# One core, attention and two gated layers in one kernel: normalising sums in two broadcasts, own buffer rings for the heads, and order edges behind the step's main work

## The chip, the cores and the metric

The kernel runs on 1 core of one Trainium2 chip. The metric is the device time of one execution in microseconds (us). The core has five engines with a queue each, worked off in order: TensorE (PE; its weight loads are shown as PEld), VectorE (DVE), ScalarE (ACT), GpSimd (POOL) and SyncE (SP), which here only issues DMAs.

## The reference, cut to what matters

Batch 4, 8 heads, sequence 1152, head size 64. Queries are pooled in pairs, so 576 remain.

```python
q_pool = q.reshape(B, H, S // 2, 2, D).mean(axis=3)
attn = softmax(q_pool @ k.T / 8)            # per head, 576 x 1152
x = concat_heads(attn @ v)                  # (4, 576, 512)
# stage 2: 4 experts of size 64, the best 2 of 4 per token weigh in
for e in range(4):
    a = softmax(causal(x @ wq[e] @ (x @ wk[e]).T / 8))
    out += gate[..., e] * (a @ (x @ wv[e]) @ wo[e])
# stage 3: previous token mixed in, then two products and a gate
k = relu(xk @ w_k); out = sigmoid(xr @ w_r) * (k * k @ w_v)
```

## The kernel before, in words

**Order of the work.** The code emits steps (`Step`: `qk` for the products on PE, `ew` and `ew2` for what follows on other engines, `pv` for the value products). `drive` (L168) goes through the list of steps; a step's `pv` runs LAG = 4 steps later. Side work is put in between: `Task(start, end, atoms)` spreads a list of small functions over a stretch of steps, and `later(n, f)` runs f n steps on. What is emitted is not yet the order on the engines: the framework's scheduler sorts all instructions at compile time with its own estimate of durations, and may put an instruction whose inputs it believes ready ahead of others that were emitted long before. `behind(ins, prev)` (L760) adds an edge without a semaphore (`NoSync`), which holds `ins` behind `prev` in that order.

**Stage 1** (`s1_job`, L767) has 32 heads of 9 steps, some 26 us each. A step multiplies one block of 128 keys with all 576 queries (L781, L782) into one of two score buffers `st`, and ACT takes the exponential (L787) into one of 10 buffers `p`. POOL and DVE add the `p` of a head up (L797, L801). Value products (L815) run after steps 2, 5 and 8 of a head; ACT copies the result out of PSUM into `U` (L824). In the next head the summed `p` is multiplied with ones (L831), and `finish2` (L846) copies these sums of the softmax into the other half of `U` (L848). A DMA spreads them over 64 partitions (`sd`, L854), DVE takes the reciprocal (L858), a DMA writes them to memory (`scr`, L859), a DMA broadcasts them back (`R`, L863: 2 groups of 64 partitions with 288 values each), and POOL multiplies `U` by `R` into `XT` (L871). `mid`, `bcast` and `end` are run by `later`, 1, 2 and 5 steps after the sums. Heads 0 and 1 take another way (`finish`, L876, and `normaliser`, L237, whose broadcast goes to 64 partitions with 576 values, L254).

For the head after next, `s1_prep` (L620) transposes keys and queries and splits them into a high and a low part (`sk`), and DMAs copy these into `KK` and `QQ` (L668, L669, L711, L712); `s1_max` (L719) multiplies again for the maximum of each row, which DVE takes (L730); `max_finish` (L393) sends it to `QQ` by DMA (L409, L410). All of these results, and the value products, share four PSUM banks (`aux`, L117).

**Stage 2** of a batch runs inside the next batch's heads: `s2_split` (L259) copies `XT` to `XH` on ACT and subtracts on DVE for `XL` (one pair of heads at a time), `s2_vproj` (L267) and `s2_qk` (L337) project, `s2_max` and `s2_job` (L419, L455) do an expert, whose end (`normaliser`, L237; `end`, L533) goes like a head's, with `mid`, `bcast` and `end` 2, 3 and 4 steps after the sums; `s2_out` (L545) is the output projection. Where these steps stand among a head's nine is written out by hand in `G` (L26): `p1` for three steps of `s2_vproj` and one of `s2_qk` in head 1 of the next batch, `po` for `s2_out` in head 0 of the batch after. The task of `s2_split` comes at step 13 counted from the start of the next batch's head 0 (L1089). The last batch's stage 2 and the weights' last chunks follow from 817 us on.

**Stage 3** reads weights that `w3_split` (L938) makes out of float64 words, in 20 chunks through one staging buffer `w3st`: a load (L947), seven small steps on DVE and ACT (L960 to L990), two stores (L993). It fills the last 226 us.

U, R, `sd` and `rd` of heads and experts come from one pool `sm` with two buffers a name.

Of the kernel before, what the change touches and what calls it, by code (L numbers as in the profile page):

```python
# [9 lines left out]
F32 = mybir.dt.float32  # L10
# [5 lines left out]
ALU = mybir.AluOpType  # L16
# [39 lines left out]
def tile_kernel(ctx: ExitStack, tc: tile.TileContext, q, k, v, w_gate, wq, wk, wv, wo,  # L56
# [5 lines left out]
    def copy(e, dst, src):  # L62
        if e == "s":
            nc.scalar.activation(dst, src, AF.Copy)  # L64
        elif e == "v":
            nc.vector.tensor_copy(dst, src)
        else:
            nc.gpsimd.tensor_scalar(dst, src, 1.0, 0.0, op0=ALU.mult, op1=ALU.add)

    def lo_of(e, dst, src, hi):  # L70
        eng[e].tensor_tensor(dst, src, hi.bitcast(F32), op=ALU.subtract)  # L71

# [80 lines left out]
    def later(n, fn):  # L153
        pending.append((now[0] + n, fn))
# [10 lines left out]

    lagged = []

    def drive(steps, tasks, drain=False, first=0):  # L168
# [67 lines left out]

    def normaliser(U, gate, name):  # L237
# [217 lines left out]
    def s2_job(pp, b, e):  # L455
# [68 lines left out]
        def finish(j):  # L524
            if j == 0:
                acc["U"] = sm.tile([P, T], F32, tag="U", name=f"U{name}")
            U = acc["U"]
            copy_eps(G["u2"], U[: D + 1, j * HT : (j + 1) * HT], acc[j][: D + 1, :HT])
            if j == 0:
                return  # L530
            mid, R = normaliser(U, GR[:, e], name)

            def end():  # L533
                o0 = (e % 2) * D
                y = U
                eng[G["y2"]].tensor_tensor(y[o0 : o0 + D], U[0:D], R, op=ALU.mult)
                copy(G["yh"], YH[o0 : o0 + D, e // 2], y[o0 : o0 + D])
# [68 lines left out]
    def s1_load(hh):  # L606
        b, h = hh // H, hh % H
        kr = s1a.tile([P, NC * D], F32, tag="kr", name=f"kr{hh}")
        qr = s1a.tile([QW, NQ, 2, D], F32, tag="qr", name=f"qr{hh}")
        raw[hh] = kr, qr  # L610
        return [
            lambda: nc.sync.dma_start(qr, q[b, h].rearrange("(c p r) d -> p c r d", p=QW, r=2)),
            lambda: nc.sync.dma_start(kr, k[b, h].rearrange("(p c) d -> p (c d)", p=P)),
        ]

    def s1_vload(hh):
        b, h = hh // H, hh % H
        return [lambda: nc.sync.dma_start(VF[hh % NF][:, :, 0:D], v[b, h].rearrange("(p c) d -> p c d", p=P))]

# [99 lines left out]
    def s1_max(hh):  # L719
# [3 lines left out]
        def one(c, g):  # L723
            t0, n = TC[c]

            def f():
                ps = aux()
                nc.tensor.matmul(ps[:n, : 3 * P], QA[i][:, t0 : t0 + n], KA[i][:, 3 * g * P : 3 * (g + 1) * P],  # L728
                                 start=True, stop=True)
                nc.vector.tensor_reduce(pm[:n, c, g : g + 1], ps[:n, : 3 * P], axis=AX.X, op=ALU.max)  # L730
            return f
# [27 lines left out]

    def behind(ins, prev):  # L760
        if prev is not None:
            tc.add_manual_dep(ins.ins, prev.ins.name,
                              mybir.DependencyInfo(mybir.DependencyClass.NoSync, mybir.DependencyReason.DATA),
                              reason="order")
        return ins

    def s1_job(hh):  # L767
# [5 lines left out]
        def make(si):  # L773
# [11 lines left out]
            def ew():  # L785
                pt = ps[si] = pp1.tile([P, 2, HT], F32, tag="p", name=f"p1_{hh}_{si}", bufs=G["PB"])
                nc.scalar.activation(pt, acc.pop(("st", si))[:, :, :HT], AF.Exp, scale=1.0 / 16.0)  # L787

            def ew2():
# [5 lines left out]
                if x is not None:  # L795
                    s = pp1.tile([P, 2, HT], F32, tag="s" + e, name=f"s{e}1_{hh}_{si}", bufs=HB)
                    eng[e].tensor_tensor(s, x, ps[si], op=ALU.add)  # L797
                    sums[e] = s
# [5 lines left out]
            def values():  # L804
# [16 lines left out]
                if si == NC - 1:  # L821
                    owed.append(total)
                    U = acc["U"] = sm.tile([P, T], F32, tag="U", name=f"U1_{hh}")
                    copy("s", U[:, :HT], a[:, :HT])  # L824
                    if hh == NH - 1:
                        owed.pop(0)(last_qk[0])
# [19 lines left out]
        def finish2(s):  # L846
            U = acc["U"]
            nc.scalar.activation(U[0 : D + 1, HT:], s[0 : D + 1, :HT], AF.Identity, bias=eps[0 : D + 1])  # L848
            sd = sm.tile([D, T // D], F32, tag="sd", name=f"sd1_{hh}")
            rd = sm.tile([D, T // D], F32, tag="rd", name=f"rd1_{hh}")  # L850
            scr = dscr.tile([1, T], F32, tag="scr", name=f"scr1_{hh}")
            R = sm.tile([P, HT], F32, tag="R", name=f"R1_{hh}")
            for j in range(2):
# [3 lines left out]
            def mid():  # L857
                nc.vector.reciprocal(rd, sd)  # L858
                nc.sync.dma_start(scr.rearrange("o (p i) -> (o p) i", p=D), rd)  # L859
                later(G["bc"], bcast)  # L860

            def bcast():
                nc.sync.dma_start(R, bass.AP(tensor=scr.tensor, offset=scr.offset, ap=[[HT, 2], [0, D], [1, HT]]))  # L863

            def end():
                o0 = (h % 2) * D
                for j in range(2):
                    a = slice(j * D, (j + 1) * D)
                    x = XT[o0 : o0 + D, h // 2].rearrange("p (t e n) -> p e t n", n=QW, e=2)[:, j]
                    y, z = (w[a].rearrange("p (t n) -> p t n", n=QW) for w in (U[:, :HT], R))  # L870
                    eng[G["xt" if b else "xt0"]].tensor_tensor(x, y, z, op=ALU.mult)  # L871

            later(G["mid"], mid)
            later(G["end1"], end)

# [62 lines left out]
    def w3_split(first, end, pool, bufs):  # L938
        def chunk(src, n):
# [47 lines left out]
            def sp7():  # L987
# [390 lines left out]
```

## Time and profile before

| what | value |
|---|---|
| median of 3 runs | 1174.4 us (1164.23 to 1182.01) |
| the profiled execution | 1168.17 us |
| its span, first to last instruction | 1166.5 us |
| mean granted clock of PE | 0.931 |
| PE, DVE, ACT, POOL busy | 1032.9, 743.9, 456.9, 383.3 us |

Busy time is time in which an engine executes; a wait is the idle time of an engine before an instruction, with the instruction that released it. The clock is the share of PE's full 2.4 GHz that was granted, and 0.50 stands for 1.2 GHz.

### The profile page before, as it was taken

The page shows a single profiled execution, that of the slowest core. Times are in us where ns is not written, and L with a number is a line of the kernel's source. Part 1 is how long each engine was busy: PE and PEld are TensorE (multiplying, and loading weights), DVE is VectorE, ACT ScalarE, POOL GpSimd, SP SyncE. Part 2 cuts the span into 40 slices and gives each one's busy share as a digit, 9 for nine tenths or more (in the row PEclk, how much of TensorE's full clock was granted, in tenths as well). Part 3 has the DMA queues.
Part 4 walks back from the last instruction along what each step waited for, and adds up shares of the span by engine and source line. Part 5 has one row for each costly group of instructions (what it writes and reads, how often), then busy time and mean ns, then how long its engine had stood idle before and what let it go on. Part 6 is the DMA issues. An engine that isn't in the chain of part 4 may idle for free. (4 is left out here: it accounts for less than half of the span.)

```text
span 1166.5 us, 17687 instructions
## 1 busy us (share of the span) xinstructions
PE 1032.9 (89%) x6186; PEld 811.2 (70%) x6186; DVE 743.9 (64%) x1501; ACT 456.9 (39%) x823; POOL 383.3 (33%) x483
## 2 busy tenths in 40 slices
PE   6998877879988789998889899998788899999998
PEld 4765555657666567766667776766776678888887
DVE  5676655576769577786867766684587644444432
ACT  5334334334445433453543434453256322222221
POOL 5156345233334442453433244434212101111110
PEclk9999888889899898998989888997889989999999
DMA  5656464445454474654536455316626421111100
GB/s 132 145 122 143 103 135 107 111 119 118 119 140 111 105 188 118 134 134 119 138 84 180 126 124 120 74 38 190 179 83 194 137 84 37 37 37 37 43 31 19
DMA packets 139655, 128.05 MB, mean 110 GB/s; under 512 B 64741, under 2 KB 103838, under 8 KB 139566
## 3 DMA queue, kind: packets, MB, share of 16 engines
q1 hardware_dynamic: 139566, 126.92, 43.8%
q8 instruction: 49, 0.80, 0.3%
q14 instruction: 40, 0.33, 0.1%
HBM read 63.24 MB, written 20.07 MB: 71 GB/s over the span
## 5 line engine op out<-in xcount | busy, mean ns | idle before, releaser
L730 DVE TENSOR_REDUCE PM<-bank 128x1 f32<-128x384 f32 (+1 forms) x390 | 205.9, 548 | 85.4 <-PE bank L728 83.6
L787 ACT ACTIVATE p<-st 128x576 f32<-128x576 f32 x288 | 184.7, 649 | 135.9 <-PE st L782 129.8
L781 PE MATMUL st<-QQ,KK 128*128 128x288 f32 x576 | 190.1, 341 | 17.4 <-ACT p L787 15.2
L728 PE MATMUL bank<-KK,QQ 128*128 128x384 f32 (+1 forms) x390 | 153.7, 419 | 42.4 <-DVE PM L730 17.7
L782 PE MATMUL st<-QQ,KK 65*128 65x288 f32 x576 | 178.3, 321 | 5.8 <-DMA QQ<-mr 5.2
L797 POOL TENSOR_TENSOR sg<-sg,p 128x576 f32<-128x576 f32 x90 | 137.1, 1523 | 117.4 <-ACT p L787 69.1
L815 PE MATMUL bank<-p,VF 128*64 128x288 f32 x1080 | 165.3, 448 | 0.0
L781 PEld LDWEIGHTS st<-QQ,KK 128*128 128x128 f32 x576 | 118.9, 207 | 41.1 <-ACT p L787 29.1
L728 PEld LDWEIGHTS bank<-KK,QQ 128*128 128x128 f32 (+1 forms) x390 | 77.6, 204 | 77.3 <-DVE PM L730 29.5
L782 PEld LDWEIGHTS st<-QQ,KK 65*128 65x128 f32 x576 | 119.8, 208 | 13.9 <-DMA QQ<-mr 5.9
L815 PEld LDWEIGHTS bank<-p,VF 128*64 128x64 f32 x1080 | 76.0, 148 | 60.2 <-issue 26.4
L871 POOL TENSOR_TENSOR XT<-U,R 64x288 f32<-64x288 f32 x60 | 49.9, 831 | 159.4 <-DMA R<-scr 140.6
L1175 PE MATMUL sth<-xkh,wk 128*128 128x256 f32 x512 | 91.4, 279 | 1.2 <-ACT relu L1182 1.2
L1175 PEld LDWEIGHTS sth<-xkh,wk 128*128 128x128 f32 x512 | 78.7, 188 | 1.8 <-ACT relu L1182 1.4
L503 PE MATMUL bank<-p,V 128*65 128x288 f32 (+5 forms) x288 | 65.9, 364 | 13.1 <-ACT U L64 6.1
L1112 POOL TENSOR_SCALAR yxr<-x,omr 128x256 f32<-128x256 f32 x36 | 26.2, 744 | 140.6 <-DVE xkl L144 130.6
L1175 PE MATMUL sth<-xkl,wk 128*128 128x256 f32 x256 | 71.4, 279 | 0.0
L797 DVE TENSOR_TENSOR sv<-sv,p 128x576 f32<-128x576 f32 x60 | 55.2, 920 | 23.1 <-PE bank L831 12.9
L489 POOL TENSOR_SCALAR_AFFINE_SELECT p<-p 128x128 f32<-128x128 f32 (+1 forms) x96 | 29.3, 336 | 115.9 <-ACT p L481 90.8
L1182 ACT ACTIVATE relu<-sth 128x512 f32<-128x512 f32 x32 | 17.5, 596 | 123.2 <-PE sth L1175 122.5
L797 POOL TENSOR_TENSOR sg<-p,p 128x576 f32<-128x576 f32 x30 | 46.4, 1546 | 52.9 <-ACT p L787 50.3
L1183 DVE TENSOR_TENSOR relu<-relu 128x512 f32<-128x512 f32 x32 | 20.9, 688 | 57.9 <-ACT relu L1182 57.9
(214 smaller groups left out, 2173.1 us busy)
## 6 DMA issues: line engine op xcount, KB each, us to landing
KK<-sk SPq DMA_DIRECT2D x30, 320.0 KB
qr<-in_q_dram SPq DMA_DIRECT2D x32, 288.0 KB
kr<-in_k_dram SPq DMA_DIRECT2D x32, 288.0 KB
VF<-in_v_dram SPq DMA_DIRECT2D x32, 288.0 KB
QQ<-sk SPq DMA_DIRECT2D x60, 144.0 KB
KK<-sk SPq DMA_DIRECT2D x30, 256.0 KB
R<-scr SPq DMA_DIRECT2D x48, 144.0 KB
w3h<-w3st SPq DMA_DIRECT2D x20, 256.0 KB
```

The lines of the kernel that those rows point to most:

```text
L489: nc.gpsimd.affine_select(o, o, pattern=[[1, o.shape[1]]], compare_op=ALU.is_ge, fill=0.0, base=m0, channel_multiplier=-1)
L503: nc.tensor.matmul(a[:, q0 + lo : q0 + hi], V2[:n, c, e], pt[:n, c0 + lo : c0 + hi], start=start, stop=stop)
L728: nc.tensor.matmul(ps[:n, : 3 * P], QA[i][:, t0 : t0 + n], KA[i][:, 3 * g * P : 3 * (g + 1) * P], start=True, stop=True)
L730: nc.vector.tensor_reduce(pm[:n, c, g : g + 1], ps[:n, : 3 * P], axis=AX.X, op=ALU.max)
L781: nc.tensor.matmul(st[:, n, :HT], KA[i][:, ks], QA[i][:, cs], start=True, stop=False)
L782: last_qk[0] = nc.tensor.matmul(st[:, n, :HT], KB[i][0 : D + 1, ks], QB[i][0 : D + 1, cs], start=False, stop=True)
L787: nc.scalar.activation(pt, acc.pop(("st", si))[:, :, :HT], AF.Exp, scale=1.0 / 16.0)
L797: eng[e].tensor_tensor(s, x, ps[si], op=ALU.add)
L815: prev = behind(nc.tensor.matmul(a[j * D : (j + 1) * D, :HT], V[:, x, 0:D], ps[x][:, j], start=si == GRP[0] and x == si, stop=si == NC - 1 ...
L871: eng[G["xt" if b else "xt0"]].tensor_tensor(x, y, z, op=ALU.mult)
L1112: nc.gpsimd.tensor_scalar(y[:, c], t[:, c, 0:GT], om[:, c : c + 1], 0.0, op0=ALU.mult, op1=ALU.add)
L1175: nc.tensor.matmul(st[:, f // 2, f % 2 * GT : (f % 2 + 1) * GT], w[kt][:, fs], x[:, kt], start=i == 0, stop=i == 3 * KT - 1)
```

## The change

Six things are done. (1) The broadcast of `finish2` is two DMAs of 64 partitions each. (2) U, `sd`, `rd` and R of heads come from the pool `pp1`, two buffers a name, and no longer share those of stage 2. (3) For all heads but the last, `mid`, `bcast` and `end` come 2, 4 and 7 steps after the sums; for experts of all batches but the last 3, 5 and 7. (4) `s2_split` is taken apart: the four pairs are copied at steps 1 and 5 of head 6, step 6 of head 7 and step 6 of the next batch's head 1, and the steps of `p1` and `po` come later. (5) `pin` ties instructions without a semaphore behind the latest exponential ("s"), the latest maximum of `s1_max` ("v") or POOL's latest add ("g"): copies out of PSUM, XH and YH copies, reciprocals, products, and the loads of q, k and v. (6) A chunk of `w3_split` has four empty atoms between its load and its first step. Of the last head and the last batch nothing is pinned or put off.

```diff
-G = {... 'mid': 1, 'bc': 1, 'end1': 5, 'mid2': 2, 'end2': 4, 'spl': 9, 'p1': (5, 5, 5, 9), 'po': (2, 4, 5, 9) ...}
+G = {... 'mid': 2, 'bc': 2, 'end1': 7, 'mid2': 2, 'end2': 4, 'mid3': 3, 'end3': 7, 'xhp': ((6, 1), (6, 5), (7, 6), (9, 6)), 'p1': (8, 8, 9, 9), 'po': (4, 5, 7, 9) ...}
+    mark = {}
+    def pin(ins, e):
+        return behind(ins, mark.get(e))
     def normaliser(U, gate, name, pinned=False):
...
-            nc.vector.reciprocal(rd, sd)
+            x = nc.vector.reciprocal(rd, sd)
+            if pinned:
+                pin(x, "v")
...
-            later(G["bc"], bcast)
+            later(G["bc"] if pinned else 1, bcast)
     def s2_split(b):
-                copy(G["xh"], XH[:, p], XT[:, p])
+                x = copy(G["xh"], XH[:, p], XT[:, p])
+                if b < B - 1:
+                    pin(x, "s")
     # s2_job, end: product pinned "v", YH copy pinned "s" if b < B - 1
-            later(G["mid2"], mid)
-            later(G["end2"], end)
+            later(G["mid3" if early else "mid2"], mid)
+            later(G["end3" if early else "end2"], end)
     # s1_load, s1_vload
-            lambda: nc.sync.dma_start(qr, ...),
+            lambda: pin(nc.sync.dma_start(qr, ...), "s"),
     # s1_max, s1_job: the instructions that are tied behind
+                mark["v"] = nc.vector.tensor_reduce(pm[:n, c, g : g + 1], ...)
+                mark["s"] = nc.scalar.activation(pt, ..., AF.Exp, scale=1.0 / 16.0)
+                    mark[e] = eng[e].tensor_tensor(s, x, ps[si], op=ALU.add)
     # values, finish2
-                    U = acc["U"] = sm.tile([P, T], F32, tag="U", name=f"U1_{hh}")
-                    copy("s", U[:, :HT], a[:, :HT])
+                    U = acc["U"] = pp1.tile([P, T], F32, tag="U", name=f"U1_{hh}", bufs=2)
+                    x = copy("s", U[:, :HT], a[:, :HT])
+                    if hh < NH - 1:
+                        pin(x, "s")
...
-                nc.sync.dma_start(R, bass.AP(tensor=scr.tensor, offset=scr.offset, ap=[[HT, 2], [0, D], [1, HT]]))
+                for j in range(2):
+                    nc.sync.dma_start(R[j * D : (j + 1) * D], bass.AP(tensor=scr.tensor, offset=scr.offset + j * HT, ap=[[0, D], [1, HT]]))
...
-            later(G["mid"], mid)
-            later(G["end1"], end)
+            later(G["mid"] if late else 1, mid)
+            later(G["end1"] if late else 5, end)
     # w3_split
-            return [ld, sp1, sp2, sp3, sp4, sp5, sp6, sp7]
+            idle = lambda: None
+            return [ld, idle, idle, idle, idle, sp1, sp2, sp3, sp4, sp5, sp6, sp7]
     # the task of s2_split
-        tasks.append(Task(at(b * H, LAG + G["spl"]), at(b * H, LAG + G["spl"] + 1), s2_split(b - 1)))
+        for f, (i, j) in zip(s2_split(b - 1), G["xhp"]):
+            tasks.append(Task(at((b - 1) * H + i, j), at((b - 1) * H + i, j) + 0.5, [f]))
```

## Rows read from the trace of the kernel before

**Rows 1.** The page: busy us, share of the span, instructions.
```profile
PE 1032.9 (89%) x6186; PEld 811.2 (70%) x6186; DVE 743.9 (64%) x1501; ACT 456.9 (39%) x823; POOL 383.3 (33%) x483
```

**Rows 2.** Waits of PE by releaser: us in total, times, longest us.
```profile
PE bank L728 <- DVE PM L730: 17.7, 16, 5.5
PE st L781 <- ACT p L787: 15.2, 10, 5.2
PE stv L280 <- ACT p L787: 7.5, 2, 3.9
PE bank L728 <- DMA KK<-sk: 6.3, 3, 3.3
PE bank L503 <- ACT U L64: 6.1, 1, 6.1
...
PE st L782 <- DMA QQ<-mr: 5.2, 2, 3.4
PE bank L728 <- ACT U L133: 5.1, 3, 3.0
...
PE stv L280 <- ACT XH L64: 4.8, 2, 3.3
...
PE bank L728 <- ACT U L64: 3.3, 1, 3.3
```

**Rows 3.** Timeline 166.9 to 178: start, us, instruction, [idle before <- releaser].
```profile
166.97 0.58 SPq L863 DMA_DIRECT2D R<-scr  x1
...
174.89 1.63 POOL L871 TENSOR_TENSOR XT<-U,R 64x288 f32<-64x288 f32 x2 [3.98 <-DMA R<-scr]
176.55 0.68 ACT L64 ACTIVATE XH<-XT 128x576 fp32r<-128x576 f32 x1 [4.94 <-POOL XT L871]
177.14 0.63 ACT L787 ACTIVATE p<-st 128x576 f32<-128x576 f32 x1
...
177.83 0.61 PE L781 MATMUL st<-QQ,KK 128*128 128x288 f32 x1 [5.24 <-ACT p L787]
```

**Rows 4.** Waits of POOL and ACT, whole run, as in rows 2.
```profile
POOL XT L871 <- DMA R<-scr: 140.6, 27, 9.6
...
ACT p L787 <- PE st L782: 129.8, 164, 4.4
...
ACT XH L64 <- POOL XT L871: 39.9, 9, 6.9
```

**Rows 5.** Timeline 810 to 814: stage 2's broadcast and its reader.
```profile
810.27 0.53 SPq L254 DMA_DIRECT2D R<-scr  x1
...
813.76 0.75 DVE L536 TENSOR_TENSOR U<-U,R 64x576 f32<-64x576 f32 x1 [1.42 <-DMA R<-scr]
```

**Rows 6.** Timeline 145 to 160: a copy of keys behind an R.
```profile
147.25 0.60 SPq L669 DMA_DIRECT2D KK<-sk  x1
...
155.57 0.66 PE L728 MATMUL bank<-KK,QQ 128*128 128x384 f32 x1 [3.29 <-DMA KK<-sk]
```

**Rows 7.** Timeline 236 to 252: DVE at a weight chunk.
```profile
244.08 0.43 DVE L961 TENSOR_SCALAR w3st<-w3st 128x512 int32<-128x512 int32 x1 [3.38 <-DMA w3st<-in_moe_w_k_dram]
```

**Rows 8.** The chain that ended last, 817 to 836: start, us, what.
```profile
826.39 6.95 DMA R<-scr
```

**Rows 9.** Fifteen half-clock stretches, sum row: us, then busy us by engine.
```profile
sum 95.50, PE 79.75 PEld 59.38 DVE 55.42 ACT 33.27 POOL 35.96; mean PE 5.32 PEld 3.96 DVE 3.69 ACT 2.22 POOL 2.40
```

**Rows 10.** Stretches: us, busy us (instructions) of PE, PEld, DVE, ACT, POOL; clock; DMA.
```profile
105.00:237.00 132.00, 108.56 (x646) 77.07 (x646) 77.33 (x150) 50.46 (x91) 54.44 (x52) 0.90 0.51 114
237.00:466.00 229.00, 196.61 (x1208) 150.12 (x1206) 166.01 (x346) 97.53 (x182) 87.27 (x101) 0.90 0.54 128
466.00:670.00 204.00, 181.21 (x1148) 139.08 (x1149) 150.58 (x318) 90.57 (x170) 79.30 (x93) 0.94 0.55 131
670.00:817.00 147.00, 134.60 (x825) 98.23 (x824) 99.49 (x206) 64.94 (x120) 61.71 (x79) 0.91 0.46 110
455.00:535.00 80.00, 73.10 (x471) 54.02 (x470) 63.90 (x137) 36.13 (x68) 32.94 (x40) 0.98 0.62 137
```

More of the change, by code (lines that the diff above doesn't have):

```diff
@@ new lines @@
+G = {'LAG': 4, 'LO': 2, 'nf1': 2, 'nfx': 1, 'mxA': (0, 5), 'mxB': (-1.0, 5.5), 'mxC': (-3.5, 5.0), 'prA': (0.5, 5.0), 'prB': (-1.5, 2.0), 'mx0': (-4.2, 4.0), 'mx1': (-4.2, 4.0), 'vl': (0.0, 1.5), 'vs': (5.5, 1.0), 'pr0': (-3.0, 1.0), 'pr1': (-3.0, 1.0), 'ldA': (5.5, 5.0), 'ldB': (2.5, 2.0), 'ld': (1.5, 1.0), 'm2': (2.0, 3.0), 'nm': 2, 'nm2': 1, 'dup': 1, 'mid': 2, 'bc': 2, 'end': 9, 'end1': 7, 'mid2': 2, 'end2': 4, 'mid3': 3, 'end3': 7, 'xhp': ((6, 1), (6, 5), (7, 6), (9, 6)), 'gate': 8, 'gate2': 2, 'w2': (2, 30), 'w3': (7, 14), 've': 'g', 'kh0': 's', 'kh1': 's', 'qh0': 's', 'qh1': 's', 'kq': 's', 'kl': 'v', 'rs': 'v', 'rl': 'v', 'ym': 'g', 'yo': 'v', 'LGe': 'v', 'p1': (8, 8, 9, 9), 'p2': (9, 9, 9), 'p3': (2,), 'p4': (9, 9, 9, 9), 'p5': (8, 8, 8, 8), 'p6': (9, 9, 9), 'po': (4, 5, 7, 9), 'add0': 'g', 'add1': 'g', 'xt': 'g', 'u1': 's', 'u2': 's', 'y2': 'v', 'yh': 's', 'yl': 'v', 'xo': 'v', 'v2': 's', 'xh': 's', 'xl': 'v', 'vvh': 's', 'vvl': 'g', 'klo': 'v', 'HB': 2, 'PB': 10, 'GRP': (2, 5, 8), 'GA': (1, 3, 5, 7), 'blk': 1, 'm2w': 2, 'order': 2, 'kdup': 0, 'L2': 4, 'O2': 1, 'a0': (5.0, 5.0), 'a1': (2.0, 2.5), 'a2': (0.0, 1.0), 'a3': (2.0, 2.0), 'r0': 2, 'NV': 2, 'NF': 2, 'ua': 'v', 'u0': 's', 'xt0': 'g', 'w3d': 8, 'w3q': (3, 27), 'WC': 1, 'kb': 1, 'kst': 1, 'qst': 0, 'CW': 512, 'wt': 'v', 'wl': 'v', 'wa': 'v', 'WB': 1, 'mxg': 4, 'hq': 's', 'hpos': (0, 1, 11, 20)}
@@ L63, in copy @@
         if e == "s":
[L64 to L68, printed above, removed]
+            return nc.scalar.activation(dst, src, AF.Copy)
+        if e == "v":
+            return nc.vector.tensor_copy(dst, src)
+        return nc.gpsimd.tensor_scalar(dst, src, 1.0, 0.0, op0=ALU.mult, op1=ALU.add)
     def lo_of(e, dst, src, hi):
-        eng[e].tensor_tensor(dst, src, hi.bitcast(F32), op=ALU.subtract)
+        return eng[e].tensor_tensor(dst, src, hi.bitcast(F32), op=ALU.subtract)
     B, H, S, _ = q.shape
@@ L166, in tile_kernel, with behind @@
     lagged = []
+    mark = {}
+    def behind(ins, prev):
+        if prev is not None:
+            tc.add_manual_dep(ins.ins, prev.ins.name,
+                              mybir.DependencyInfo(mybir.DependencyClass.NoSync, mybir.DependencyReason.DATA),
+                              reason="order")
+        return ins
+    def pin(ins, e):
+        return behind(ins, mark.get(e))
     def drive(steps, tasks, drain=False, first=0):
@@ L235, in tile_kernel, with normaliser @@
     pp_last = None
-    def normaliser(U, gate, name):
+    def normaliser(U, gate, name, pinned=False):
         NI = T // D
@@ L530, in finish @@
                 return
-            mid, R = normaliser(U, GR[:, e], name)
+            early = b < B - 1
+            mid, R = normaliser(U, GR[:, e], name, early)
             def end():
@@ L535, in end @@
                 y = U
-                eng[G["y2"]].tensor_tensor(y[o0 : o0 + D], U[0:D], R, op=ALU.mult)
-                copy(G["yh"], YH[o0 : o0 + D, e // 2], y[o0 : o0 + D])
+                x = eng[G["y2"]].tensor_tensor(y[o0 : o0 + D], U[0:D], R, op=ALU.mult)
+                z = copy(G["yh"], YH[o0 : o0 + D, e // 2], y[o0 : o0 + D])
+                if early:
+                    pin(x, "v")
+                    pin(z, "s")
                 lo_of(G["yl"], YL[o0 : o0 + D, e // 2], y[o0 : o0 + D], YH[o0 : o0 + D, e // 2])
-            later(G["mid2"], mid)
-            later(G["end2"], end)
+            later(G["mid3" if early else "mid2"], mid)
+            later(G["end3" if early else "end2"], end)
         return [make(si) for si in range(3)]
@@ L611, in s1_load @@
         return [
-            lambda: nc.sync.dma_start(qr, q[b, h].rearrange("(c p r) d -> p c r d", p=QW, r=2)),
-            lambda: nc.sync.dma_start(kr, k[b, h].rearrange("(p c) d -> p (c d)", p=P)),
+            lambda: pin(nc.sync.dma_start(qr, q[b, h].rearrange("(c p r) d -> p c r d", p=QW, r=2)), "s"),
+            lambda: pin(nc.sync.dma_start(kr, k[b, h].rearrange("(p c) d -> p (c d)", p=P)), "s"),
         ]
@@ L617, in s1_vload @@
         b, h = hh // H, hh % H
-        return [lambda: nc.sync.dma_start(VF[hh % NF][:, :, 0:D], v[b, h].rearrange("(p c) d -> p c d", p=P))]
+        return [lambda: pin(nc.sync.dma_start(VF[hh % NF][:, :, 0:D], v[b, h].rearrange("(p c) d -> p c d", p=P)), "s")]
     def s1_prep(hh):
@@ L729, in f @@
                                  start=True, stop=True)
-                nc.vector.tensor_reduce(pm[:n, c, g : g + 1], ps[:n, : 3 * P], axis=AX.X, op=ALU.max)
+                mark["v"] = nc.vector.tensor_reduce(pm[:n, c, g : g + 1], ps[:n, : 3 * P], axis=AX.X, op=ALU.max)
             return f
@@ L758, in tile_kernel @@
     last_qk, owed = [None], []
[L760 to L765, printed above, removed]
     def s1_job(hh):
@@ L796, in ew2 @@
                     s = pp1.tile([P, 2, HT], F32, tag="s" + e, name=f"s{e}1_{hh}_{si}", bufs=HB)
-                    eng[e].tensor_tensor(s, x, ps[si], op=ALU.add)
+                    mark[e] = eng[e].tensor_tensor(s, x, ps[si], op=ALU.add)
                     sums[e] = s
@@ L847, in finish2 @@
             U = acc["U"]
-            nc.scalar.activation(U[0 : D + 1, HT:], s[0 : D + 1, :HT], AF.Identity, bias=eps[0 : D + 1])
-            sd = sm.tile([D, T // D], F32, tag="sd", name=f"sd1_{hh}")
-            rd = sm.tile([D, T // D], F32, tag="rd", name=f"rd1_{hh}")
+            late = hh < NH - 1
+            x = nc.scalar.activation(U[0 : D + 1, HT:], s[0 : D + 1, :HT], AF.Identity, bias=eps[0 : D + 1])
+            if late:
+                pin(x, "s")
+            sd = pp1.tile([D, T // D], F32, tag="sd", name=f"sd1_{hh}", bufs=2)
+            rd = pp1.tile([D, T // D], F32, tag="rd", name=f"rd1_{hh}", bufs=2)
             scr = dscr.tile([1, T], F32, tag="scr", name=f"scr1_{hh}")
-            R = sm.tile([P, HT], F32, tag="R", name=f"R1_{hh}")
+            R = pp1.tile([P, HT], F32, tag="R", name=f"R1_{hh}", bufs=2)
             for j in range(2):
@@ L857, in mid @@
             def mid():
-                nc.vector.reciprocal(rd, sd)
+                x = nc.vector.reciprocal(rd, sd)
+                if late:
+                    pin(x, "v")
                 nc.sync.dma_start(scr.rearrange("o (p i) -> (o p) i", p=D), rd)
-                later(G["bc"], bcast)
+                later(G["bc"] if late else 1, bcast)
             def bcast():
-                nc.sync.dma_start(R, bass.AP(tensor=scr.tensor, offset=scr.offset, ap=[[HT, 2], [0, D], [1, HT]]))
+                for j in range(2):
+                    nc.sync.dma_start(R[j * D : (j + 1) * D], bass.AP(tensor=scr.tensor, offset=scr.offset + j * HT, ap=[[0, D], [1, HT]]))
             def end():
@@ L870, in end @@
                     y, z = (w[a].rearrange("p (t n) -> p t n", n=QW) for w in (U[:, :HT], R))
-                    eng[G["xt" if b else "xt0"]].tensor_tensor(x, y, z, op=ALU.mult)
-            later(G["mid"], mid)
-            later(G["end1"], end)
+                    x = eng[G["xt" if b else "xt0"]].tensor_tensor(x, y, z, op=ALU.mult)
+                    if late:
+                        pin(x, "g")
+            later(G["mid"] if late else 1, mid)
+            later(G["end1"] if late else 5, end)
         def finish(j):
```

5 lines of the change are left out of this document (2 added, 3 removed).

## The prediction, before the result was known

> **What bounds the kernel now.** I read the page's busy shares first, then TensorE's own waits, then one of its longest stalls in order of time, then who released the engines in it, and last the stages side by side. TensorE (PE) is busy 89% of the span [rows 1], so only what holds PE up can pay. Of PE's 134 us without work, nine rows of its waits name 71 [rows 2]: ACT is the releaser in six of them (15.2 + 7.5 + 6.1 + 5.1 + 4.8 + 3.3 = 42.0 us), a landing DMA in two (6.3 + 5.2 = 11.5), DVE's maximum in one (17.7).
>
> One stall in full [rows 3]: SP issues the broadcast R<-scr at 166.97; POOL, idle for 3.98, starts the product XT only at 174.89, so the broadcast took about 7.8 us; ACT has the copy XH<-XT at the front of its queue and stands still for 4.94; the exponential behind it starts at 177.14, though its scores were ready; PE, which needs a free score buffer, stood for 5.24. Over the run POOL waits 140.6 us for R and ACT 39.9 for XT in nine copies [rows 4]. POOL's own waiting costs nothing. What ACT passes on does. The code emits this copy only after head 8, and it runs here right behind head 5's product: the scheduler pulled it ahead of exponentials as soon as that product was due by its own reckoning. That is the disease of this kernel: small instructions that wait for a far transfer sit in front of an in-order engine's main work.
>
> **The change, part by part.**
>
> *Broadcast in two.* The 128-partition broadcast takes 7.8 us [rows 3]. The stage-2 one, of as many bytes on 64 partitions out of one row, is issued at 810.27 and releases DVE at 813.76, 3.5 us [rows 5]. Two transfers of 64 partitions are each like it with half the bytes, issued 0.58 apart [rows 3]; bounds 1.8 (half of 3.5) and 7.8 + 0.58; I take 3.5 + 0.6 = 4.1, nearest to the like row, 3.7 less. Price: 30 more issues on SP at 0.58, 17 us of a queue that other DMAs stand in; PE sees them only where the next DMA is one that it waits for.
>
> The Trainium skill, "DMA: Bandwidth & Descriptors", section on the anatomy of one DMA, gives about 2.0 us plus bytes over 436 GB/s (fitted on the POOL path) and advises fewer, larger transfers: an estimate from that page is 2.3 us for the one transfer and 2 x 2.2 for two in series, so the split would lose 2 us per head. The trace disagrees on its first term, 7.8 where the page gives 2.3. The same page, section on why a DMA's semaphore goes up by 16, says that the slowest dimension of both sides sets how many of 16 engines work: 2 before, 16 after; that sides with the 3.5.
>
> *Neighbours of R.* KK<-sk, issued at 147.25, three issues behind an R, released PE at 155.57, 8.3 us [rows 6]. If R leaves its engines 4 us sooner, so does what queues there: the 11.5 us of KK and QQ<-mr. Bounds 0 and 11.5.
>
> *Later middle and end.* In wide heads reciprocal, broadcast and product come 2, 4 and 7 steps after the sums instead of 1, 2 and 5: still three steps from broadcast to product, which at some 26 us per head of 9 to 13 steps are 6 to 8 us, against 4.1. In stage 2 they come at 3, 5, 7 instead of 2, 3, 4: two steps, 4 to 5 us. The last head keeps 1, 2, 5. Results come at most three steps later and are read later still (next point): nothing, with 0 to 3 us at each of three batch ends as bounds.
>
> *XH copies moved and pinned.* The twelve early copies (0.68 each, [rows 3]) go to heads 6, 6, 7 and the second head of the next batch. Head 7's product falls near step 4 of that head, its copy stands at 6, and the projection that reads it goes from 5 to 8: two steps each. No work is added. So the nine ACT stalls [rows 4] lose their cause, but for the last batch's.
>
> *Own rings.* U, sd, rd and R of the heads no longer share two buffers with stage 2. That takes away the evictions U (L133) that waited for XT: 5.1 us of PE [rows 2].
>
> These two parts: 42.0, less 1.4 of stv<-XH that belongs to the unpinned last batch, and 2.4 of st<-p (ten waits, the longest 5.2; my estimate of the short ones in it): 38.2 us. What is late next is the exponential's real input, and DVE.
>
> *Pins on DVE, SP and POOL.* Reciprocals stand behind a maximum, loads behind an exponential, products behind an add. They are order edges without a semaphore, so a load adds no wait at run time; it leaves its place ahead of QQ<-mr in SP's queue. *Idle atoms:* a weight chunk gets four empty slots between its load and its first operation; DVE stood 3.38 us before that operation for the load [rows 7], and a maximum queued behind it. Of DVE's 17.7 I take half, 8.9 (bounds 0 and 17.7): the scheduler may still pull these unpinned operations forward.
>
> *Last head.* Its R is on the chain that ended last, 6.95 us [rows 8]; 4.1 instead gives 2.9.
>
> *The clock.* I took fifteen stretches that begin at or around such gaps and have a granted clock of 0.50, the 1.2 GHz level: 95.5 us together, PE busy in 79.75 of them [rows 9]. At 2.4 GHz the busy part would halve: 39.9 us.
>
> The skill's "TensorE: Matmul & The Clock Gate", section Terms, sets the loss at the throttled time times what is missing of the clock: 47.8 by that estimate, where my row gives 39.9, since PE idled in the rest. The sum would be lower by 4 at half weight.
>
> **Sum.** 38.2 + 11.5 + 8.9 + 2.9 = 61.5 of idle and 39.9 of clock, 101.4 if all is kept. All is not kept, for the stages show a floor [rows 10]. The quietest 80 us (455 to 535, clock 0.98) still idle 6.9, 8.6%. Idle of the stages: 23.4 of 132, 32.4 of 229, 22.8 of 204, 12.4 of 147. Brought to 8.6% they lose 12.0, 12.7, 5.3 and 0: 30, half of 61.5. I keep half of both, 30.7 + 20.0, and take 3 off for the issues and late results: 47.7. From the profiled execution's own 1168.2 (span 1166.5 and 1.7 around it): **1120 us**. The median of three runs is 1174.4; the profiled run is 0.5% faster, so this is 4.6% under the median. About 2% is what a measurement of this kernel tells from no change: 1151 and 1198.
>
> **Rivals.**
>
> *All of it is kept* (10%): 1168.2 - 101.4 = 1067. For it: the stalls named are most of the idle time in 105 to 237. Against: the floor of 8.6%.
>
> *DVE takes over* (17%): the reciprocals pinned behind maxima and the maxima themselves become what PE waits for. For: its maximum is the largest single releaser of PE [rows 2], and each of them has PE queued behind it. Against: over three batches DVE is busy 166 + 151 + 99 of 580 us [rows 10], 72%. Price: half of ACT's and DMA's 49.7 and the last head's 2.9 are won (27.8), the 17.7 of DVE double, the clock drops stay: 1168.2 - 27.8 + 17.7 = 1158.
>
> *Two transfers land no sooner than one* (5%), by whatever holds them: XT still waits, but XH does not stand behind it; half of 38.2 and half of that in clock, 28.7, less 17 of issues: 1157. The skill's rule on batching, named above, would have it so. The change would then not do its first part.
>
> *A pinned eviction holds a bank* (11%): slower. The copies of values and sums out of PSUM (58 in the 29 pinned heads) now stand behind an exponential. That waits for PE's scores, on average 129.8/164 = 0.79 us [rows 4], and takes 0.63 [rows 3]. PE in turn needs one of four banks for its maxima and values (the rows bank<-U in rows 2 show it waiting so). If each passes 1.42 on, that is 82 us: 1120 + 82 = 1202. It decides against the change from 34 of the 58 on (47.7/1.42). Against it: these copies run in step with exponentials already.
>
> *Nothing moves* (2%): 1168.
>
> **How the numbers follow.** The forecast has 55%, with a range of its own of 1095 to 1150 (73 down to 18 of the 101 us kept). Faster by over 2%: 0.53 of the forecast, 0.10, a quarter of the DVE case 0.04 and 0.03 of the two transfers, 0.70. Within 2%: 0.02 + 0.13 + 0.02 + 0.02, 0.19. Slower: 0.11. The range is from 1080 to 1165: it leaves out most of the best case and the slower one.
>
> **What would show it.** Right: the wait XT<-R falls from 140.6 to under 40; ACT's wait XH<-XT is nearly gone; KK no longer appears in PE's waits; the mean granted clock rises from 0.931 to 0.95 or more; PE's rows with ACT as releaser sum to under 20. Wrong: XT<-R stays over 100 (transfers), DVE PM passes 35 in PE's waits (DVE), or bank<-U passes 20 (pins). A clock that stays at 0.93 with less idle time would leave 1140.

## The result and the profile after

The changed kernel takes 1092.66 us (median of four runs, 1089.83 to 1092.99), the kernel before, on the same chip, 1178.2 us (four runs, 1164.23 to 1184.06). The ratio is 0.934, 95% interval 0.927 to 0.941: faster, inside the range of 1080 to 1165, 27 us below the forecast of 1120 and just under the forecast's own range of 1095 to 1150. The ratio compares fast runs alone: two of the four runs of the kernel before, 1182.01 and 1184.06, are over 1.5% above its fastest and are left out, so it isn't the quotient of the two medians. The profiled execution took 1092.36 us.

The page of after, its first line on busy time; the line beside its core gives span and clock:

```profile
PE 999.7 (92%) x6186; PEld 785.7 (72%) x6186; DVE 752.8 (69%) x1501; ACT 454.6 (42%) x823; POOL 396.1 (36%) x483
```

```profile
core 0: 1090.7 us, clock 0.965
```

PE has the same 6186 instructions and is busy 999.7 us instead of 1032.9 [rows 1]. These 33.2 us are put down to the clock (0.931 to 0.965), since the work is the same; 42.6 came from PE's idle time: 1166.5 - 1032.9 = 133.6 before, 1090.7 - 999.7 = 91.0 now. The sum is the 75.8 us that the span lost.

Who still holds PE up, in after's waits of PE by releaser (us in total, times, longest us):

```profile
PE st L792 <- ACT p L798: 7.1, 14, 1.7
PE bank L746 <- DVE PM L748: 6.4, 13, 1.3
PE sth L1259 <- ACT relu L1267: 6.2, 1, 6.2
PE bank L746 <- DVE PM L762: 5.3, 7, 1.8
...
PE bank L517 <- ACT p L495: 4.6, 1, 4.6
...
PE st L793 <- DMA QQ<-ml: 0.2, 1, 0.2
```

Against rows 2: the row of KK<-sk is gone and so is that of QQ<-mr; DVE's maximum fell from 17.7 to 6.4 with a longest wait of 1.3 instead of 5.5; PE's wait for an exponential fell from 15.2 to 7.1. The 6.2 in stage 3 is new, and comes back below.

The same view for POOL and ACT, where rows 4 were 140.6 and 39.9:

```profile
POOL XT L890 <- DMA R<-scr: 52.0, 16, 9.7
...
ACT XH L64 <- POOL XT L890: 3.2, 3, 1.4
```

One broadcast in time order, as the timeline of after shows it (start, us, instruction, idle before it and its releaser). It is to be held against rows 3:

```profile
203.21 1.12 SPq L882 DMA_DIRECT2D R<-scr  x2
...
206.18 0.79 POOL L890 TENSOR_TENSOR XT<-U,R 64x288 f32<-64x288 f32 x1 [1.27 <-DMA R<-scr]
...
207.32 0.79 POOL L890 TENSOR_TENSOR XT<-U,R 64x288 f32<-64x288 f32 x1 [0.36 <-DMA R<-scr]
...
208.15 0.68 ACT L64 ACTIVATE XH<-XT 128x576 fp32r<-128x576 f32 x1 [1.39 <-POOL XT L890]
```

Two issues lie in one row (x2, 1.12 us together). The first half releases POOL 2.97 us after 203.21, the second 4.11 us after it; before, the one transfer took about 7.8 us. ACT stands 1.39 us in front of its copy, where rows 3 show 4.94.

Stretches of after, all in stage 1 (us, busy us and instructions of PE, PEld, DVE, ACT, POOL; clock; DMA share; GB/s):

```profile
105.00:230.00 125.00, 115.68 (x730) 82.68 (x731) 92.89 (x186) 58.99 (x107) 62.96 (x61) 0.97 0.63 145
230.00:445.00 215.00, 202.97 (x1364) 154.78 (x1360) 179.67 (x368) 106.33 (x200) 98.54 (x114) 1.00 0.57 140
445.00:635.00 190.00, 176.26 (x1147) 133.39 (x1148) 157.14 (x316) 88.79 (x167) 86.29 (x93) 0.97 0.58 141
```

In the middle stretch PE idles 215 - 202.97 = 12.0 us, 5.6%, at a clock of 1.00. The 8.6% that the prediction took for a floor [rows 10] was none.

### The profile page after: what moved, and what is told of

Read it like the earlier page. It is cut to its first block, busy times and chain, and to the rows that moved or that the text cites. A ratio compares the mean times of both kernels' runs of the same rounds, so it can differ in the third digit from the quotient of the medians.

```text
span 1090.7 us, 17718 instructions
## 1 busy us (share of the span) xinstructions
PE 999.7 (92%) x6186; PEld 785.7 (72%) x6186; DVE 752.8 (69%) x1501; ACT 454.6 (42%) x823; POOL 396.1 (36%) x483
## 4 chain that ended last, share of the span: by engine, by line
PE 58%; DVE 22%; DMA 9%; ACT 5%; issue 3%; POOL 2%; SPq 1%; DVEq 0%; ACTq 0%; POOLq 0%
PE stw L1234 9%; PE bank L826 8%; PE sth L1198 7%; PE st L792 5%; DVE PM L748 5%; PE bank L746 5%; PE st L793 4%; PE str L1221 4%; PE stq L361 3%; DVE sv L808 2%; PE bank L517 2%; DMA R<-scr 2%; PE bank L853 2%; PE sto L573 2%; DMA scr<-rd 1%
## 5 line engine op out<-in xcount | busy, mean ns | idle before, releaser
L792 PE MATMUL st<-QQ,KK 128*128 128x288 f32 x576 | 182.0, 330 | 10.0 <-ACT p L798 7.1
L793 PE MATMUL st<-QQ,KK 65*128 65x288 f32 x576 | 169.6, 308 | 0.2 <-DMA QQ<-ml 0.2
L808 POOL TENSOR_TENSOR sg<-sg,p 128x576 f32<-128x576 f32 x90 | 134.3, 1492 | 91.0 <-ACT p L798 59.1
L826 PE MATMUL bank<-p,VF 128*64 128x288 f32 x1080 | 155.7, 427 | 0.8 <-DVE PM L748 0.8
L792 PEld LDWEIGHTS st<-QQ,KK 128*128 128x128 f32 x576 | 112.2, 195 | 36.6 <-ACT p L798 19.8
L793 PEld LDWEIGHTS st<-QQ,KK 65*128 65x128 f32 x576 | 112.6, 196 | 7.4 <-issue 4.9
L746 PEld LDWEIGHTS bank<-KK,QQ 128*128 128x128 f32 (+1 forms) x390 | 75.0, 197 | 54.3 <-DVE PM L748 19.6
L826 PEld LDWEIGHTS bank<-p,VF 128*64 128x64 f32 x1080 | 72.2, 141 | 55.2 <-issue 17.8
L890 POOL TENSOR_TENSOR XT<-U,R 64x288 f32<-64x288 f32 x60 | 59.3, 988 | 57.1 <-DMA R<-scr 52.0
L517 PE MATMUL bank<-p,V 128*65 128x288 f32 (+5 forms) x288 | 59.5, 333 | 8.7 <-ACT p L495 4.6
L1206 DVE TENSOR_TENSOR relu<-relu 128x512 f32<-128x512 f32 x32 | 20.8, 687 | 55.9 <-ACT relu L1205 55.9
```

Of the source, the lines that this page charges most:

```text
L517: nc.tensor.matmul(a[:, q0 + lo : q0 + hi], V2[:n, c, e], pt[:n, c0 + lo : c0 + hi], start=start, stop=stop)
L792: nc.tensor.matmul(st[:, n, :HT], KA[i][:, ks], QA[i][:, cs], start=True, stop=False)
L793: last_qk[0] = nc.tensor.matmul(st[:, n, :HT], KB[i][0 : D + 1, ks], QB[i][0 : D + 1, cs], start=False, stop=True)
L808: mark[e] = eng[e].tensor_tensor(s, x, ps[si], op=ALU.add)
L826: prev = behind(nc.tensor.matmul(a[j * D : (j + 1) * D, :HT], V[:, x, 0:D], ps[x][:, j], start=si == GRP[0] and x == si, stop=si == NC - 1 ...
L890: x = eng[G["xt" if b else "xt0"]].tensor_tensor(x, y, z, op=ALU.mult)
```

## The experiments

Two theories stood at first. Theory A is the prediction's: the gain comes from the moved and tied copies and the own rings, because ACT no longer stands in front of a late XT. Theory B: the gain comes from the broadcast in two transfers. Ratios are to the kernel before on the same chip, with their 95% interval.

**The split alone, put into the kernel before.**

```diff
-                nc.sync.dma_start(R, bass.AP(..., ap=[[HT, 2], [0, D], [1, HT]]))
+                for j in range(2):
+                    nc.sync.dma_start(R[j * D : (j + 1) * D], bass.AP(..., offset=scr.offset + j * HT, ap=[[0, D], [1, HT]]))
```

> The kernel before with only the broadcast of a head's reciprocals cut into two transfers of 64 partitions. Theory A (the ACT copies that sit ahead of exponentials are the cause, the slow broadcast only their length): the copies still sit there, but each wait is some 4 us shorter, so about a third to a half of the whole gain of 78 us, 1135 to 1152 us. Theory B (the broadcast on few DMA engines is the cause, with the transfers queued behind it): nearly all of it, 1095 to 1115 us. POOL's wait XT<-R falls from 140.6 to under 60 by both; ACT's wait XH<-XT falls from 39.9 to 10 to 20.

1090.35 us, 0.927 (0.923 to 0.931): the whole gain and, if anything, more, under the range of either theory. Of all waits, POOL's and ACT's for these tiles, and PE's for DVE's maximum:

```profile
POOL XT L872 <- DMA R<-scr: 34.1, 12, 5.5
...
ACT XH L64 <- POOL XT L872: 15.6, 9, 3.0
...
PE bank L728 <- DVE PM L730: 10.2, 12, 2.9
```

The copies stand where they stood and ACT still waits nine times, for 15.6 us instead of 39.9. PE's idle time is 1092.9 - 1005.5 = 87.4 us. By its size the gain is Theory B's.

**The changed kernel with one broadcast.** The reverse of the edit above, put into after.

> The changed kernel with the broadcast as one transfer of 128 partitions again, all else kept. Theory A: PE's ACT-released waits stay small, since nothing of ACT stands behind the product; KK and QQ come late again: 1100 to 1120 us. Theory B: most of the gain goes, 1140 to 1165 us. By both POOL's wait XT<-R goes up to over 100.

1146.82 us, 0.975 (0.971 to 0.979), in Theory B's range. So the rest of the change, on a slow broadcast, is worth 2.5%; on a fast one it adds nothing that can be measured in sum (two of its parts, of opposite sign, come below). The gains do not add up: both parts shorten the same wait of ACT, which is a likely reason and not a tested one. Of all waits, POOL's and ACT's for these tiles:

```profile
POOL XT L889 <- DMA R<-scr: 139.9, 28, 12.4
...
ACT XH L64 <- POOL XT L889: 10.0, 3, 5.4
```

R is as late as before, and ACT's XH copies wait 10.0 us for the product instead of 39.9. Yet PE idles 1148.6 - 1029.0 = 119.6 us, and only 14.0 of the 133.6 are won.

**The changed kernel without its order edges.**

```diff
     def pin(ins, e):
-        return behind(ins, mark.get(e))
+        return ins
```

> The changed kernel without any of the order edges of pin, all else kept (two transfers, rings, later steps, moved copies, idle atoms). Theory A: the scheduler pulls the XH copies forward again, behind a product that now comes 2 steps later, and with R 4 us sooner: half of the gain is lost, 1120 to 1145 us, ACT's wait XH<-XT above 10. Theory B: at most 10 us are lost, 1092 to 1103 us.

1086.98 us, 0.923 (0.919 to 0.927), again under the range of either theory. The wait of ACT's XH copies for XT is 12.9 us instead of 3.2, and no time is lost by it. The edges bring no time.

**The moved and tied XH copies alone, in the kernel before.** The last pair's copy comes at step 4 of head 1, not 6, and `p1` and `po` stay where they were.

```diff
-                copy(G["xh"], XH[:, p], XT[:, p])
+                x = copy(G["xh"], XH[:, p], XT[:, p])
+                if b < B - 1:
+                    pin(x, "s")
...
-        tasks.append(Task(at(b * H, LAG + G["spl"]), ..., s2_split(b - 1)))
+        for f, (i, j) in zip(s2_split(b - 1), ((6, 1), (6, 5), (7, 6), (9, 4))):
+            tasks.append(Task(at((b - 1) * H + i, j), at((b - 1) * H + i, j) + 0.5, [f]))
```

> The kernel before with only the twelve XH copies moved to steps of their own (6,1), (6,5), (7,6), (9,4) and tied behind the exponential. Theory A: the stalls in which PE waited for ACT with XH ahead (about 33 us with the clock stretches behind them another 15 to 20) go, half kept: 1135 to 1150 us, ACT's wait XH<-XT under 8. Theory B: the broadcast stays slow and the wait only moves, 1160 to 1180 us.

1162.53 us, 0.989 (0.985 to 0.992), in Theory B's range. PE's waits by releaser:

```profile
PE bank L740 <- DMA KK<-sk: 15.1, 5, 3.6
PE bank L740 <- DVE PM L742: 13.8, 14, 5.5
PE bank L740 <- ACT U L132: 9.2, 5, 3.4
...
PE st L787 <- DMA QQ<-ml: 7.1, 6, 4.0
```

The XH copies' wait for XT halved (39.9 to 18.9), and PE's idle time stayed: 1161.1 - 1028.7 = 132.4. PE's wait for exponentials fell (st<-p from 15.2 to 7.1), and others rose: ACT's evictions U from 5.1 to 9.2, and above all a landing DMA, KK, from 6.3 [rows 2] to 15.1. That is the line which points at the transfers beside R.

So a second pair was set up. Theory L: the late R itself costs, through XT. Theory N: the slow transfer costs because it holds others up that are issued after it.

**The split, and the old broadcast once more into a tile that nobody reads.** R is early, the slow transfer is still there.

```diff
+            RX = pp1.tile([P, HT], F32, tag="RX", name=f"RX_{hh}", bufs=1) if hh < NH - 2 else None
...
+                if hh < NH - 2:
+                    nc.sync.dma_start(RX, bass.AP(..., ap=[[HT, 2], [0, D], [1, HT]]))
```

> The kernel before with the broadcast in two transfers of 64 partitions, and behind them, for heads 2 to 29, the old 128-partition broadcast once more into a tile that nobody reads. R itself lands early, but what is issued next queues behind the old transfer. Theory L (R's own landing is what counts, through XT, XH and U): close to the split alone, 1090 to 1105 us. Theory N (the copies to KK and QQ and the loads that queue behind it count): most of the gain goes, 1140 to 1170 us, and KK<-sk is again among PE's waits. By both POOL's wait XT<-R stays under 50.

1148.33 us, 0.978 (0.973 to 0.982), in Theory N's range. PE's waits by releaser:

```profile
PE bank L728 <- DMA KK<-sk: 14.8, 5, 3.5
...
PE bank L429 <- DMA KA<-KA: 11.6, 5, 5.8
...
PE st L782 <- DMA QQ<-ml: 6.1, 3, 3.7
PE st L782 <- DMA QQ<-mr: 5.2, 4, 3.7
```

Four rows, all of landing DMAs, make 37.7 us. One such case in the timeline of this kernel:

```profile
171.38 1.19 SPq L865 DMA_DIRECT2D R<-scr  x2
172.62 0.56 SPq L867 DMA_DIRECT2D RX<-scr  x1
...
173.77 0.64 SPq L668 DMA_DIRECT2D KK<-sk  x1
174.22 2.08 POOL L875 TENSOR_TENSOR XT<-U,R 64x288 f32<-64x288 f32 x2 [0.18 <-DMA R<-scr]
174.45 0.60 SPq L669 DMA_DIRECT2D KK<-sk  x1
...
182.68 0.66 PE L728 MATMUL bank<-KK,QQ 128*128 128x384 f32 x1 [3.12 <-DMA KK<-sk]
```

R's first half is there after 2.84 us. The second KK copy, three issues behind RX, reaches PE 8.2 us after its own issue (174.45), as in rows 6 (8.3), and nobody reads RX.

What holds it is in the trace too, which has the time of every update of a transfer's semaphore. This KK copy has 16: the 14th came 3.66 us after its issue, the last two at 8.11 and 8.13. RX has just two late updates, at 7.46 and 7.48. The late pairs come in the order of issue: RX, QQ, KK, KK and the load of q are complete 7.5, 8.0, 9.5, 10.0 and 10.7 us after the issue of RX. In the kernel before it is the same. Of 120 KK copies, 60 were issued while an R was in flight: at the median their 14th update came at 3.5 us, the 15th at 7.8, the last at 8.0, and the other 60 copies were complete at 3.4. So a neighbour is late by as many updates as the slow transfer itself has, and by their order it stands behind that transfer.

**The control: the same extra bytes, in the fast form.**

```diff
-                if hh < NH - 2:
-                    nc.sync.dma_start(RX, bass.AP(..., ap=[[HT, 2], [0, D], [1, HT]]))
+                for j in range(2 if hh < NH - 2 else 0):
+                    nc.sync.dma_start(RX[j * D : (j + 1) * D], bass.AP(..., ap=[[0, D], [1, HT]]))
```

> The control to the run with an old broadcast into an unread tile: the same extra bytes for the same heads, but as two transfers of 64 partitions. If it is the bytes that cost, about as slow as that run, 1140 to 1155 us; if it is that the old form holds few DMA engines, near the split alone, 1088 to 1105 us, with no KK<-sk above 5 us among PE's waits.

1117.21 us, 0.953 (0.950 to 0.956): between the ranges of both theories, a miss for either. PE's waits by releaser:

```profile
PE bank L728 <- DVE PM L730: 12.8, 15, 2.7
...
PE bank L429 <- DMA KA<-KA: 3.0, 2, 2.0
```

The row of KK under bank is gone, KK is complete 3.5 us after its issue at the median, and KA<-KA is 3.0 instead of 11.6. Of the 5.1 points that the idle slow transfer gave back (0.927 to 0.978), 2.4 are its form; the other 2.6 come with extra transfers of these bytes and issues, or with the order that the scheduler makes of them, which no run separates.

**A late R in the fast form.** The two transfers go into a spare tile, and a copy brings it to R one step later.

```diff
-                nc.sync.dma_start(R, ...)
+                for j in range(2):
+                    nc.sync.dma_start((RT if RT is not None else R)[j * D : (j + 1) * D], ...)
+                if RT is not None:
+                    later(1, lambda: nc.sync.dma_start(R, RT))
```

> The kernel before with the broadcast in two transfers into a spare tile and a copy of this tile into R one step later, for heads 2 to 29. R lands some 3 to 5 us later than with the split alone, about as late as before, but nothing holds two DMA engines for 4 us. Theory L: the product and what stands behind it are late as before, 1140 to 1170 us. Theory N: near the split alone, 1090 to 1110 us. By both POOL's wait XT<-R is over 90.

1105.99 us, 0.943 (0.938 to 0.948), in Theory N's range. The expected wait for R over 90 us did not come; of all waits, POOL's and ACT's for these tiles:

```profile
POOL XT L875 <- DMA R<-RT: 21.7, 11, 7.2
ACT U L133 <- POOL XT L875: 21.7, 8, 5.7
...
ACT XH L64 <- POOL XT L875: 10.9, 5, 3.4
```

The scheduler, it seems, counted the copy in and placed the product later. From the reciprocal's end to the first of a head's two products it is 10.9 us at the median by the trace, against 10.2 before and 6.6 in the split alone: R is used as late as before, and 5.7 of 7.3 points of gain stay. R's lateness and the extra copy cost 1.6 points together here. But a product that is late by plan is not one that is late by surprise. ACT waits 32.6 us for XT in all (10.9 and 21.7), against 19.7 in the split alone (15.6 and 4.1 for U) and 60.4 before (39.9 and 20.5), so the ACT stalls of rows 3 are tested by this only in part.

**Earlier steps in the changed kernel** (mid, bcast and end back to 1, 1 and 5, for experts to 2, 3 and 4):

```diff
-'mid': 2, 'bc': 2, 'end1': 7, 'mid3': 3, 'end3': 7
+'mid': 1, 'bc': 1, 'end1': 5, 'mid3': 2, 'end3': 4
```

> The changed kernel with reciprocal, broadcast and product at 1, 2 and 5 steps (experts 2, 3 and 4) as before the change, all else kept. If the later steps matter with the fast broadcast, waits for R grow and the time goes up by 10 to 20 us; if, as the split alone suggests, they do not, it stays within 6 us of 1092.7.

1104.41 us, 0.940 (0.935 to 0.944), DVE's maximum in PE's waits at 12.6 instead of 6.4. The interval overlaps that of after in the first result (0.927 to 0.941), but not that of the same kernel run again, 0.931 (0.928 to 0.933, below): the medians are 11.5 us apart, in the range that was expected if the later steps matter, and POOL's wait for R grew as expected, from 52.0 to 64.4. In the changed kernel they are thus worth about 1%, which is also what a new order alone moved the time by (the reservation below). The split alone has early steps too and is at 0.927, so they aren't needed for this time; why they count in the one and not in the other is open.

**The last two heads out of the early-closing pool.** In after PE loses 6.2 us at the start of stage 3. Timeline of after:

```profile
739.55 1.09 SPq L882 DMA_DIRECT2D R<-scr  x2
742.17 1.65 POOL L890 TENSOR_TENSOR XT<-U,R 64x288 f32<-64x288 f32 x2 [3.73 <-DMA R<-scr]
743.85 0.60 ACT L1267 ACTIVATE relu<-sth 128x512 f32<-128x512 f32 x1 [7.72 <-POOL XT L890]
...
744.50 0.58 PE L1259 MATMUL sth<-xkh,wk 128*128 128x256 f32 x1 [6.20 <-ACT relu L1267]
```

Stage 3's relu has nothing to do with the last head's XT by its data. The reading: `pp1` closes at the end of stage 1, its space goes to later tiles, and so they wait for the last reader of U and R. In the kernel before, U and R were in `sm`, which lives on. With one broadcast the same wait was 12.5 us (in the changed kernel with one broadcast), so it follows R.

```diff
-                    U = acc["U"] = pp1.tile([P, T], F32, tag="U", name=f"U1_{hh}", bufs=2)
+                    U = acc["U"] = (pp1.tile(..., bufs=2) if hh < NH - 2 else sm.tile(...))
...
```

(`sd`, `rd` and R likewise.)

> The changed kernel with U, sd, rd and R of the last two heads in the pool that stays open (as before the change), all else kept. My theory: the 6.2 us in which PE waits for a relu of stage 3 came from the own rings: stage 3's tiles lie where the closed pool lay and wait for the last head's product. That wait goes and the time falls by 4 to 7 us, to 1086 to 1089 us. Rival: the wait is passed on to the last batch's projection, which needs the same product, and the time stays within 2 us of 1092.7.

1088.04 us, 0.928 (0.923 to 0.934); PE's wait:

```profile
PE sth L1259 <- ACT relu L1267: 0.4, 1, 0.4
```

The wait went as expected; the time is not told apart from after by this pair. So both were run again side by side, and a third without the order edges:

> The changed kernel once more, beside the two others on the same chip: 1090 to 1096 us, the measure for a difference under 1%.

> The changed kernel with the last two heads' buffers in the pool that stays open, again: if the 6.2 us wait of stage 3 is really saved, 4 to 7 us under the changed kernel on this chip; if its single runs of 1080 to 1094 us were only spread, within 3 us of it.

> The changed kernel without order edges and with the last two heads' buffers in the pool that stays open. If both effects seen before are real and add (no pins -6 us, last two heads -4 us), 1080 to 1086 us; if they are the spread of two good schedules, 1086 to 1095 us, the same as the changed kernel on this chip.

| kernel | median us | ratio (95%) | runs |
|---|---|---|---|
| after, again | 1092.92 | 0.931 (0.928 to 0.933) | 5 |
| last two heads in `sm` | 1083.15 | 0.924 (0.921 to 0.928) | 6 |
| the same, no order edges | 1080.2 | 0.922 (0.918 to 0.925) | 6 |

The first two intervals just touch, at 0.928; the medians are 9.8 us apart, and 4.6 in the first pair, and four of the six runs in `sm` are below the fastest of after (1087.64). So the pool costs time, here more than the 4 to 7 us that were expected; why more than the wait itself isn't shown. The third is the fastest that was found, some 1.2% below after, and its interval overlaps that of the second: the edges again bring nothing that can be told.

**A reservation for all of these.** Each edit lets the scheduler sort anew. By the order of instructions in the two traces, some 2.2% of PE's and 11% of DVE's change places between the kernel before and the split alone. Between after and after without edges it is 2.4% and 8.5%, and the time moves by 1%; so a new order by itself was small there. Between the idle slow and the idle fast transfer it is 2.5% and 8.8%, so a part of their 2.4 points can be order. An order frozen across the experiments wasn't tried.

## Why the prediction was right and where it was wrong

**Direction and the price of the broadcast: right.** 4.1 us were forecast for two transfers, from the stage-2 row [rows 5]; the timeline of after has 2.97 for the first and 4.11 for the second. The linear cost in the Trainium skill, "DMA: Bandwidth & Descriptors", section "Anatomy of one DMA", by which the split would lose 2 us a head (an estimate from that page), does not hold here: 0.927 for the split alone. The table in "Rules for kernel authors" of the same page of the Trainium skill has a line on each side: not to bother with two transfers to disjoint partition halves, and to keep a small outermost dimension, such as a leading broadcast, out of a transfer, since it confines it to at most as many engines. The runs side with the second: in the trace of before a head's R has two late updates of its semaphore, and stage 2's has sixteen.

**The step that failed is the attribution in the sum:** "These two parts: ... 38.2 us" for moved copies and own rings, against "Bounds 0 and 11.5" for neighbours of R. The experiments turn it round. The split alone gives 7.3% (1175.7 - 1090.35 = 85.4 us); all the rest, on a slow broadcast, 2.5% (1175.7 - 1146.82 = 28.9 us); the XH copies 1.1%; the edges, on a fast broadcast, nothing. By the sum the split had 14.4 us of idle time, 11.5 for the neighbours and 2.9 for the last head, before half was struck off; alone it freed 46. That the total still fell inside the range is luck in part: the sum gave too little to the split and too much to the rest. The prediction credited the split with nothing in the ACT stalls, though it shortens them (39.9 to 15.6), and counted of the neighbours only the waits where the profile names a DMA as PE's releaser. A late KK, QQ or load can also be passed on by DVE's maximum, and by ACT: in the split alone DVE's maximum is at 10.2 us instead of 17.7, with no edit to DVE's work, though its order changed. From the semaphore updates in the trace of before, KK took 8.0 us at the median where it was issued while an R was in flight and 3.4 elsewhere, QQ<-sk 7.4 and 2.5; in after KK is at 3.4. The chain "R late, XT late, XH late" was seen rightly in rows 3, but it was one instance of a wider fault.

How much is neighbours, how much R's own lateness, is bracketed loosely. That the neighbours are late is shown; what they cost has two readings. The form alone, in a transfer that nobody reads and against equal bytes, is 2.4 points (28 us), a part of which can be order. With a late R in the fast form 5.7 points (67 us) stay, which is the neighbours' share if an R late by plan costs as much as one late by surprise; that was not tested. By the first reading up to 4.9 points can be R's own lateness. Which of KK, QQ, KA and the loads carries the neighbours' share was not separated.

**"I keep half of both": wrong, and the reason for the size.** 42.6 of 61.5 us of idle (69%) and 33.2 of 39.9 of clock (83%) were kept: 75.8 instead of 30.7 + 20.0 - 3 = 47.7. The floor of 8.6% was read from the quietest 80 us of a kernel in which transfers were held up behind each R; it is 5.6% over 215 us now. No run shows the 3 us for issues by themselves. The later steps, put at nothing, are worth some 11 us in the changed kernel, a new order included.

**The cost of the own rings: missed.** The prediction put only a gain to them. They bring a wait of 6.2 us at the start of stage 3, and some 10 us of time by the second pair of runs. The prediction had no row for it, since it did not ask what takes the place of the pool's space.

**The signs.** Right: KK gone; XH<-XT 39.9 to 3.2; clock 0.965; DVE's maximum under 35; no pinned eviction holds a bank (the rows bank<-U come to 1.2 us), so the slower rival falls, and without the edges the kernel is no slower (0.923). Missed: XT<-R is 52.0, not under 40; the edges don't cause it (60.6 without), nor the later steps (64.4 with early ones), while the split alone has 34.1; the cause stays open, and POOL's own waiting costs nothing by itself. The rows of PE with ACT as releaser sum to 31.5 us, not under 20 (52.7 before, small rows included), and would stay over 20 without the new stage-3 wait too. DVE does not take over, nor are the two transfers as late as one.

## What to carry to other kernels

When a small transfer takes more than twice as long as one of like bytes, look at what is issued after it, not only at who reads it: here the copies behind it took 8.0 us instead of 3.4, and an unread transfer in the slow form cost 2.4 points more than the same bytes in the fast form. Waits for a DMA in the profile can say too little of what slow transfers cost: PE's summed to 20.8 us before, and the split alone freed 46 us of its idle time (133.6 to 87.4). An idle copy of the suspect, once in its slow form and once in its fast form, prices it. Where tiles move to another pool, ask when that pool ends and what is put in its place.

## What the runs showed of the hardware

A broadcast of 2 groups of 64 partitions took 7.8 us to its reader, and two of 64 partitions 2.97 and 4.11; and a DMA issued three places behind the first form reached PE 8.2 us after its own issue, in a kernel where nobody reads what that transfer brings. Of its 16 semaphore updates only the last two were late, at 8.1 us against 3.66 for the 14th, and the slow form has two late ones itself. The Trainium skill's "DMA: Bandwidth & Descriptors", section "Queues, rings and completion order", says that each DMA engine takes the descriptors of a queue in ring order; the late pairs, which came in the order of issue, agree with that.

More of the clock came back (83% of the forecast's full sum) than of the idle time (69%): with 42.6 us of idle gone, PE's same 6186 instructions took 33.2 us less.
